# Soft-MoE kernel on one core: stage-2 chunks set between linear steps, dispatch spectra turned on chip

## The chip, the core and the metric

One core of a Trainium2 chip runs the whole program. The metric is device time in microseconds (us), from launch to end; the profile adds one execution taken apart by engine. TensorE does matmuls, VectorE (DVE) and ScalarE (ACT) read its results out of PSUM, GpSimd (POOL) works on SBUF alone, SyncE (SP) issues most DMAs. Each engine works through its own list in order and waits on semaphores for the others.

## What is computed

The reference, cut:

```python
X = np.fft.rfft(x, axis=1)                     # x: (8, 3072, 256)
Yr = Xr @ w_r - Xi @ w_i + b_r                 # complex linear step
Yi = Xr @ w_i + Xi @ w_r + b_i
Yr, Yi = soft_threshold(Yr, 0.01), soft_threshold(Yi, 0.01)
y = np.fft.irfft(Yr + 1j * Yi)                 # (8, 3072, 256) -> 24576 rows
logits = y @ phi                               # 32 slots
d = softmax over rows;  slot_input = d.T @ y   # 8 experts, 4 slots each
slot_out = relu(slot_input @ w1[e]) @ w2[e]
c = softmax over slots; z = c @ slot_out
h = z @ w_in;  out = (h * tanh(softplus(h))) @ w_out
```

## The kernel before

The spectral part takes about the first third, the feed-forward part (the lines behind 820) the rest. Only the spectral part is touched. It goes through eight batches (b = 0 to 7), each in four steps, k = 4b to 4b + 3; a step holds eight residues q of the transform. In outline, for a batch:

- Stage 1 (line 186): six groups of matmuls; ScalarE copies them to `a`, and SP stores them to DRAM, `sdr` (line 216). SP loads `bt` from there, one load a step (line 221, `load_b`, two buffers).
- Stage 2 (line 224): for step k, six chunks (two halves h of the channels, residues in groups of 3, 3 and 2). A chunk's matmuls go to a PSUM bank; ScalarE copies it, rounded, to `xh` (line 240) and VectorE writes what is left over to `xl` (line 241). Both hold two buffers. In a batch's first step, two bins that are real are copied in SBUF as well, on VectorE, once for `xh` and once for `xl` (line 244).
- Linear (line 247): six linear steps for step k, two output halves times three products m. Each is six matmuls, three that read half 0 of `xh` and `xl` and three that read half 1. For m = 0 ScalarE copies the result; for m = 1 and 2 VectorE adds (line 277), ScalarE makes two passes (lines 283, 284) and GpSimd subtracts (line 285) into `yt`. The tile `cl` has one buffer, so ScalarE's first pass waits for GpSimd's subtraction of the linear step before.
- Then `project` (line 290, the logits' spectrum), `inv1` (line 301) and `ytrans` (line 313, y turned by TensorE).
- Once a batch: the inverse transform of the logits (`sturn`, `inv2`), both softmaxes (`smax1` to `smax3`, `csoft1`, `cexp`, `csoft2`), and the forward transform of the dispatch weights: `fwd1` (line 425), `d_load` (line 442), `fwd2` (line 472), `dturn` (line 482), and `slots` (line 487), which sums y with them.

For batches 0 to 6, `fwd1` copies its two results on ScalarE, and SP writes them to DRAM (`ddr`, line 440); `d_load` is one DMA that reads them back with the residues turned onto another axis, in runs of 128 bytes (line 445). Batch 7 has another path: VectorE transposes PSUM in blocks of 32 x 32 into `dm` (line 433), TensorE turns that (line 453), and ScalarE and VectorE copy one half each (lines 458, 456).

The order of the work is written out by hand: every piece has a position (`at`, line 75), the pieces are sorted by it, and each engine's list follows that order. Step k's linear steps stand at k, k + 1/6, ..., k + 5/6; stage 2 of step k stands at k - 1.1, its six chunks 0.0002 apart, so all before linear step (k - 1, 0) and one step ahead of their use; `load_b` at k - 1.91; stage 1's groups in batch 1 at 4.05 - 3.9 + 0.195 (2i + 1), the last at 2.295. `fwd1` stands at 4b + 5.84, `d_load` at 4b + 6.05, `fwd2` at 4b + 6.46 to 6.76. The numbers are in `PA` (line 798) and, for the last batch, `TAIL` (line 801). All PSUM tiles of this part share eight banks, handed round in the order of the program.

Of the kernel before, what the change touches and what calls it, by code (L numbers as in the profile page):

```python
# [8 lines left out]
F32 = mybir.dt.float32  # L9
# [3 lines left out]
AF = mybir.ActivationFunctionType  # L13
# [6 lines left out]
N1, N2 = 128, 24  # L20
R1, R2 = 64, 48
NP = 32
NC = 384
NS = 32
# [44 lines left out]
def body(ctx, tc, x, w_r, w_i, b_r, b_i, phi, w1, w2, w_in, w_out, cbig, ct, out, dbg=None, stop=False):  # L69
    nc = tc.nc  # L70
    NB = x.shape[0]
# [3 lines left out]
    def at(pos, fn, *a):  # L75
        items.append((round(pos, 4), len(items), fn, a))

    dram = ctx.enter_context(tc.tile_pool(name="dram", bufs=1, space=DRAM))
# [3 lines left out]
    f1, f1t, ident, sel = cb[:, 0:128], cb[:, 128:256], cb[:, 256:384], cb[:, 384:416]  # L82
# [7 lines left out]
    def lpool(name, bufs=1, **k):  # L90
        return left.enter_context(tc.tile_pool(name=name, bufs=bufs, **k))
# [3 lines left out]

    const, yp, cp, sm = lpool("const"), lpool("yp", PA["y"]), lpool("cp"), lpool("sm", 2)
    bp = ctx_r.enter_context(tc.tile_pool(name="bp", bufs=2, side="right"))
# [6 lines left out]
    def psum(shape, name):  # L104
        return psp.tile(shape, F32, tag="p", name=name)
# [17 lines left out]
    cs_t = {}  # L123

    x_t, b_t, xh_t, xl_t, yt_t, y_t, pt_t, k1_t = {}, {}, {}, {}, {}, {}, {}, {}
    sdr, spt, ddr, ch, a_t = {}, {}, {}, {}, {}
    XC = 512
    na = N2 * D // XC

# [94 lines left out]
    def stage2(k, h, p0):  # L224
        b, g = divmod(k, 4)
        n = min(3, 8 - p0)
        if h == 0 and p0 == 0:
            xh_t[k] = bp.tile([128, 2, 3 * NC + 48], F32R, tag="xh", name="xh")
            xl_t[k] = bp.tile([128, 2, 3 * NC + 48], F32R, tag="xl", name="xl")
        full = psum([128, 3, 3, 48], "s2")  # L230
        ps = full[:, 0:n]
        for i in range(n):
            nc.tensor.matmul(ps[:, i], lhsT=b_t[k][:, p0 + i, h * 128:(h + 1) * 128], rhs=t_m[:, 8 * g + p0 + i, :],  # L233
                             start=True, stop=True)

        def part(t):
            return t[:, h, 144 * p0:144 * (p0 + n)].rearrange("p (q r f) -> p q r f", r=3, f=48)

        xh = part(xh_t[k])
        nc.scalar.activation(out=xh, in_=ps, func=AF.Copy)  # L240
        nc.vector.tensor_sub(part(xl_t[k]), ps, xh.bitcast(F32))  # L241
        if g == 0 and p0 == 0:
            for t in (xh_t[k], xl_t[k]):
                nc.vector.tensor_copy(t[:, h, 3 * NC:3 * NC + 48].rearrange("p (a r) -> p a r", r=2),
                                      t[:, h, 95:144:48][:, None, :].to_broadcast([128, 24, 2]).bitcast(F32))

    def linear(k, eh, m):
        if eh == 0 and m == 0:
# [176 lines left out]
    def fwd1(b):  # L425
        d = ch[b, 1]
        last = b == NB - 1
        dm = cp.tile([128, 32, N2] if last else [128, N2, NS], F32, tag="st" if last else "chl", bufs=1 if last else 2, name="dm")
        for i in range(2):
            ps = psum([128, 12, NS], "dps")  # L430
            nc.tensor.matmul(ps, lhsT=f1, rhs=d[:, 12 * i:12 * i + 12], start=True, stop=True)
            if last:
                nc.vector.transpose(out=dm.rearrange("p q n -> p n q")[:, 12 * i:12 * i + 12], in_=ps)
            else:
                nc.scalar.activation(out=dm[:, 12 * i:12 * i + 12], in_=ps, func=AF.Copy)
        if last:
            ch[b, 0] = dm
            return
        ddr[b] = dram.tile([NP, 96, NS], F32, tag="ddr", bufs=2, name="ddr")
        nc.sync.dma_start(out=ddr[b].rearrange("q (r n) s -> (q r) n s", r=4), in_=dm)  # L440

    def d_load(b):
        if b < NB - 1:
            dd = cp.tile([96, NP, NS], F32, tag="dd", name="dd")
            nc.sync.dma_start(out=dd, in_=ddr[b].rearrange("q p s -> p q s"))
            ch[b, 0] = [dd[:, q] for q in range(NP)]
            return
        src = ch[b, 0].rearrange("p (c r) n -> p c (r n)", r=4)
        ch[b, 0] = [None] * NP
        for a in range(2):  # L450
            ps = psum([96, 4, 128], "td")
            for c in range(4):
                nc.tensor.transpose(ps[:, c], src[:, 4 * a + c], ident)
            dd = yp.tile([96, 4, 128], F32, tag="y", name="dd")
            if a:
                nc.vector.tensor_copy(dd, ps)
            else:
                nc.scalar.activation(out=dd, in_=ps, func=AF.Copy)
            for c in range(4):
                for g in range(4):  # L460
                    ch[b, 0][8 * g + 4 * a + c] = dd[:, c, 32 * g:32 * g + 32]
# [102 lines left out]
    def s1pos(b, j):  # L564
        if b < 2:
            return -5 + 0.05 * j if b == 0 else 0.15 + 0.195 * j
        if b == 2:
            return 2.5 + 0.305 * j
        return 4 * b + PA["s1"] + PA["s1d"] * j

# [10 lines left out]
    for k in range(NK):  # L581
        at(-4 + 0.01 * k if k < 2 else 2.45 if k == 4 else k + PA["lb"], load_b, k)
        for i, (h, p0) in enumerate((h, p0) for h in range(2) for p0 in (0, 3, 6)):
            at(k + PA["s2"] + PA["s2d"] * i, stage2, k, h, p0)
        for i in range(6):
            at(k + i / 6, linear, k, i // 3, i % 3)
        at(k + PA["pj"], project, k)
        at(k + PA["pj"] + 0.3, inv1, k)
        for c in range(3):
            at(k + PA["yt"] + PA["ytd"] * c if k < NK - 4 else NK + TAIL["yt"][k - NK][c], ytrans, k, c)  # L590
    def pos(n, b):
        t = TAIL.get((n, b - NB))
        return 4 * b + 4 + PA[n] if t is None else NK + t

    for b in range(NB):
        f2 = pos("f2", b)
        for n, f in (("tu", sturn), ("i2", inv2), ("m1", smax1), ("m2", smax2), ("m3", smax3), ("f1", fwd1), ("c1", csoft1),
                     ("ce", cexp), ("ds", dsum), ("dl", d_load), ("c2", csoft2)):
            at(pos(n, b), f, b)
        for g in range(4):  # L600
            at(f2 + 0.1 * g if b < NB - 1 else NK + TAIL["f2"][g], fwd2, b, g)
            at(f2 + 0.1 * g + 0.15 if b < NB - 1 else NK + TAIL["dt"][g], dturn, b, g)
        if b < NB - 2:
            at(pos("sl", b), slots, b)
        else:
            for g in range(4):
                at(NK + TAIL["sl"][b - NB][g], slots, b, (g,))
        for g in range(2):
            at(pos("cx", b) + PA["cxd"] * g, ctrans, b, g)
# [23 lines left out]
    with tc.manual_schedule():  # L633
# [11 lines left out]
        ps = psum([128, 2, NS], "sip")  # L645
# [149 lines left out]
                nc.vector.tensor_copy(sot[:, h, 16 * g:16 * g + 16].rearrange("p (j i) -> p j i", i=SPE), src)  # L795


PA = dict(y=20, s1=-5.89, s1d=0.3402, lb=-1.91, s2=-1.1, s2d=0.0002, pj=1.18, yt=2.24, ytd=0.0002, tu=0.482, i2=1.17, m1=1.17, m2=1.34, m3=1.51, f1=1.84, c1=1.58, ce=1.58, ds=2.47, dl=2.05, c2=2.57, f2=2.46, sl=3.2, rc=0.3, cx=3.24, cxd=0.0002, x0=-0.79, x1=0.05, ytl=1.05, x2=1.3, x3=2.7)


TAIL = {
# [172 lines left out]
```

## Time and profile before

| what | us |
|---|---|
| median of 3 runs | 1934.07 (1930.87 to 1936.53) |
| the profiled execution | 1935.8 |
| its span, first to last instruction | 1934.0 |
| busy in the span: TensorE | 1875.3 (97%) |
| VectorE | 1163.1 (60%) |
| ScalarE | 860.5 (44%) |
| GpSimd | 195.3 (10%) |

Busy times are sums over the whole span; a stage's own limit has to be read from that stage. A TensorE that is busy need not run at its peak, and its granted clock has two levels, 1.2 and 2.4 GHz, shown as 0.50 and 1.00. In a row, "x32" counts instructions, a pair in square brackets is the engine's idle time in front of the row and what ended it, and an fp32 matmul shows as two instructions.

### The profile page before, as it was taken

What the parts mean: (1) busy time and instruction counts of PE and PEld (TensorE: products, weight loads), DVE (VectorE), ACT (ScalarE), POOL (GpSimd) and SP (SyncE); (2) the same over time, 40 slices, a digit from 0 to 9 for tenths busy, and PEclk for the clock granted to TensorE, in tenths of its full rate; (3) what the DMA queues carried; (4) which work ended last, traced back from release to release, by engine and by line L of the source; (5) the groups of instructions that cost most, each with busy time, mean ns of one, the idle gap of its engine ahead of it and who ended that gap; (6) DMA issues with size and microseconds to landing.
All of it is one profiled execution on the core that took longest, in us unless ns stands there. A gap on an engine that the chain in (4) does not pass through costs nothing.

```text
span 1934.0 us, 29831 instructions
## 1 busy us (share of the span) xinstructions
PE 1875.3 (97%) x12106; PEld 1569.4 (81%) x12106; DVE 1163.1 (60%) x1810; ACT 860.5 (44%) x1380; POOL 195.3 (10%) x247
## 2 busy tenths in 40 slices
PE   6899999998998899999999999999999999999999
PEld 4687787777887488888888888888888888888887
DVE  3355655655566476666666666666666666666665
ACT  2666666665754243333333333333333333333332
POOL 0333333332332000000000000000000000000000
PEclk9999999999999999999999999999999999999999
DMA  9867777775663920020020020002002001000000
GB/s 246 235 150 173 168 184 177 170 185 132 161 167 107 343 74 22 23 55 22 12 55 23 23 55 23 23 12 55 22 23 55 22 19 48 22 23 22 23 22 23
DMA packets 96905, 164.28 MB, mean 85 GB/s; under 512 B 28784, under 2 KB 58096, under 8 KB 94848
## 3 DMA queue, kind: packets, MB, share of 16 engines
q1 hardware_dynamic: 93808, 155.13, 29.2%
q0 software_dynamic: 1792, 4.76, 0.8%
q10 hardware_dynamic: 1168, 2.49, 0.5%
q8 instruction: 95, 1.56, 0.3%
q14 instruction: 42, 0.34, 0.1%
HBM read 98.78 MB, written 63.57 MB: 84 GB/s over the span
## 4 chain that ended last, share of the span: by engine, by line
PE 88%; DMA 4%; DVE 3%; ACT 2%; issue 2%; POOL 1%; SPq 0%; POOLq 0%; ACTq 0%; DVEq 0%
PE o L910 56%; PE h L868 9%; PE l L265 8%; PE s L233 6%; PE tr L318 2%; PE s L201 2%; DMA dd<-ddr 2%; DMA bt<-sdr 1%; PE pp L296 1%; DMA xc<-in_x_dram 1%; PE sps L496 1%; POOL yt L285 1%; PE dt L478 1%; ACT cl L283 1%; PE iu L307 1%
## 5 line engine op out<-in xcount | busy, mean ns | idle before, releaser
L910 PE MATMUL o<-whl,gh 128*128 128x512 f32 x3072 | 1082.9, 395 | 0.0
L910 PE MATMUL o<-whl,gl 128*128 128x256 f32 x3072 | 827.9, 280 | 0.0
L881 ACT ACTIVATE g<-h 128x1024 f32<-128x1024 f32 (+1 forms) x385 | 394.2, 1025 | 747.8 <-PE h L868 738.0
L910 PEld LDWEIGHTS o<-whl,gh 128*128 128x128 f32 x3072 | 566.5, 188 | 121.5
L910 PEld LDWEIGHTS o<-whl,gl 128*128 128x128 f32 x3072 | 578.5, 188 | 31.5
L894 DVE TENSOR_TENSOR gl<-g,gh 128x1024 fp32r<-128x1024 f32 x383 | 468.9, 1224 | 29.2 <-DVE gh L887 1.4
L887 DVE CAST gh<-g 128x1024 fp32r<-128x1024 f32 (+1 forms) x385 | 265.8, 690 | 352.6 <-ACT g L881 352.6
L868 PE MATMUL h<-ctt,mst 128*128 128x512 f32 x768 | 240.7, 394 | 1.5 <-ACT g L881 1.0
L233 PE MATMUL s<-tall,bt 96*128 96x144 f32 x1024 | 143.0, 301 | 23.0 <-DMA bt<-sdr 12.1
L233 PEld LDWEIGHTS s<-tall,bt 96*128 96x128 f32 x1024 | 138.6, 202 | 31.0 <-issue 26.4
L241 DVE TENSOR_TENSOR xl<-s,xh 128x432 fp32r<-128x432 f32 (+1 forms) x192 | 94.6, 550 | 113.6 <-ACT xh L240 113.3
L285 POOL TENSOR_TENSOR yt<-cl,p 128x384 f32<-128x384 f32 x124 | 125.2, 1010 | 352.6 <-ACT p L284 220.2
L868 PEld LDWEIGHTS h<-ctt,mst 128*128 128x128 f32 x768 | 121.0, 188 | 19.7 <-ACT g L881 1.8
L283 ACT ACTIVATE cl<-p,tup 128x384 f32<-128x384 f32 x124 | 76.3, 615 | 134.0 <-DVE p L277 98.1
L918 DVE TENSOR_TENSOR os<-o,os 128x256 f32<-128x256 f32 x192 | 76.5, 419 | 77.2 <-ACT os L917 77.2
L277 DVE TENSOR_TENSOR p<-l,k 128x384 f32<-128x384 f32 x128 | 70.6, 553 | 85.2 <-PE l L265 61.9
L240 ACT ACTIVATE xh<-s 128x432 fp32r<-128x432 f32 (+1 forms) x192 | 79.0, 503 | 36.7 <-PE s L233 36.3
L917 ACT ACTIVATE os<-o 128x256 f32<-128x256 f32 x192 | 73.4, 383 | 41.5 <-PE o L910 37.7
L284 ACT ACTIVATE p<-p,tlo 128x384 f32<-128x384 f32 x124 | 76.3, 615 | 4.0
L201 PE MATMUL s<-xc,f 64*64 64x512 f32 x384 | 56.6, 650 | 9.6 <-DMA xc<-in_x_dram 9.5
L318 PEld LDWEIGHTS tr<-cb,yt 128*128 128x128 f32 x384 | 55.4, 235 | 12.0 <-issue 4.5
L318 PE MATMUL tr<-cb,yt 128*128 128x128 f32 x384 | 62.2, 306 | 0.0
(187 smaller groups left out, 1392.1 us busy)
## 6 DMA issues: line engine op xcount, KB each, us to landing
sdr<-a SPq DMA_DIRECT2D x96, 256.0 KB, 3.8
bt<-sdr SPq DMA_DIRECT2D x32, 768.0 KB, 8.5
out_dram<-os SPq DMA_DIRECT2D x47, 512.0 KB, 2.6
xc<-in_x_dram SPq DMA_DIRECT2D x90, 256.0 KB, 5.4
ctt<-c_d SPq DMA_DIRECT2D x28, 384.0 KB, 7.0
w1t<-in_moe_w_dram SPq DMA_DIRECT2D x6, 1024.0 KB, 7.4
c_d<-chl SPq DMA_DIRECT2D x14, 384.0 KB, 2.8
w2t<-in_moe_w_dram SPq DMA_DIRECT2D x5, 1024.0 KB, 12.2
```

Source lines behind the costliest of these rows:

```text
L201: nc.tensor.matmul(ps[h][64 * c:64 * c + 64], lhsT=f64[hs], rhs=t[hs, XC * c:XC * c + XC], start=True, stop=True, tile_position=(64 * h, 6 ...
L233: nc.tensor.matmul(ps[:, i], lhsT=b_t[k][:, p0 + i, h * 128:(h + 1) * 128], rhs=t_m[:, 8 * g + p0 + i, :], start=True, stop=True)
L241: nc.vector.tensor_sub(part(xl_t[k]), ps, xh.bitcast(F32))
L265: nc.tensor.matmul(full[:, 0:48 * nq].rearrange("p (q f) -> p q f", f=48), lhsT=ww[:, h, es], rhs=spec(xx, h), start=n == 0, stop=n == 5)
L283: nc.scalar.activation(out=cl, in_=p, func=AF.Relu, bias=tup[:, ri, eh:eh + 1])
L285: nc.gpsimd.tensor_sub(yt[:, eh, :, ri, :], cl, p)
L318: nc.tensor.transpose(ps[:, i, eh], yt[:, eh].rearrange("p q r f -> p (q r f)")[:, 2 * c + i::6], ident)
L868: nc.tensor.matmul(ps[:, i], lhsT=mst[:, f * 128:f * 128 + 128], rhs=ct_t[b][:, 4 * m:4 * m + 4].rearrange("p n t -> p (n t)"), start=True ...
L881: nc.scalar.activation(out=v(g), in_=v(h), func=AF.Mish)
L887: nc.vector.tensor_copy(v(gh), v(g))
L894: nc.vector.tensor_sub(gl, g, gh.bitcast(F32))
L910: nc.tensor.matmul(o, lhsT=a[:, i, ts], rhs=w, start=f == 0 and n == 0, stop=f == 15 and n == 1)
```

## The change

Three edits. Stage 2's chunks are spread: the first stands at k - 1.03 and each next one 1/6 later, so one stands in front of each of the linear steps of step k - 1. Batches 0 to 6 take the path that batch 7 had (transposes by VectorE and TensorE, `d_load` at 4b + 6.20 instead of 6.05), and the DRAM tensor and its two DMAs a batch are gone. The real bins are read from PSUM: ScalarE writes `xh`'s, VectorE subtracts for `xl`'s.

```diff
@@ stage2 @@
         if g == 0 and p0 == 0:
-            for t in (xh_t[k], xl_t[k]):
-                nc.vector.tensor_copy(t[:, h, 3 * NC:3 * NC + 48].rearrange("p (a r) -> p a r", r=2),
-                                      t[:, h, 95:144:48][:, None, :].to_broadcast([128, 24, 2]).bitcast(F32))
+            bins = full.rearrange("p q r f -> p (q r f)")[:, 95:144:48][:, None, :].to_broadcast([128, 24, 2])
+            xh, xl = (t[:, h, 3 * NC:3 * NC + 48].rearrange("p (a r) -> p a r", r=2) for t in (xh_t[k], xl_t[k]))
+            nc.scalar.activation(out=xh, in_=bins, func=AF.Copy)
+            nc.vector.tensor_sub(xl, bins, xh.bitcast(F32))
@@ fwd1 @@
-        dm = cp.tile([128, 32, N2] if last else [128, N2, NS], F32, tag="st" if last else "chl", bufs=1 if last else 2, name="dm")
+        dm = cp.tile([128, 32, N2], F32, tag="st" if last else "chl", bufs=1 if last else 2, name="dm")
         for i in range(2):
             ps = psum([128, 12, NS], "dps")
             nc.tensor.matmul(ps, lhsT=f1, rhs=d[:, 12 * i:12 * i + 12], start=True, stop=True)
-            if last:
-                nc.vector.transpose(out=dm.rearrange("p q n -> p n q")[:, 12 * i:12 * i + 12], in_=ps)
-            else:
-                nc.scalar.activation(out=dm[:, 12 * i:12 * i + 12], in_=ps, func=AF.Copy)
-        if last:
-            ch[b, 0] = dm
-            return
-        ddr[b] = dram.tile([NP, 96, NS], F32, tag="ddr", bufs=2, name="ddr")
-        nc.sync.dma_start(out=ddr[b].rearrange("q (r n) s -> (q r) n s", r=4), in_=dm)
+            nc.vector.transpose(out=dm.rearrange("p q n -> p n q")[:, 12 * i:12 * i + 12], in_=ps)
+        ch[b, 0] = dm
@@ d_load @@
         if b < NB - 1:
-            dd = cp.tile([96, NP, NS], F32, tag="dd", name="dd")
-            nc.sync.dma_start(out=dd, in_=ddr[b].rearrange("q p s -> p q s"))
-            ch[b, 0] = [dd[:, q] for q in range(NP)]
-            return
+            both = cp.tile([96, 2, 4, 128], F32, tag="dd", name="dd")
         src = ch[b, 0].rearrange("p (c r) n -> p c (r n)", r=4)
         ...
-            dd = yp.tile([96, 4, 128], F32, tag="y", name="dd")
+            dd = both[:, a] if b < NB - 1 else yp.tile([96, 4, 128], F32, tag="y", name="dd")
@@ PA @@
-s2=-1.1, s2d=0.0002, dl=2.05
+s2=-1.03, s2d=1 / 6, dl=2.2
```

## Rows read from the trace of the kernel before

**Rows 1.** Stretches: length, busy time (instructions) of each engine, clock, DMA.
```profile
0.00:640.00 640.00, 592.22 (x4826) 472.29 (x4826) 353.02 (x807) 387.17 (x788) 193.85 (x246) 0.97 0.69 178
640.00:1934.00 1294.00, 1283.10 (x7282) 1097.09 (x7281) 810.11 (x1004) 473.33 (x593) 1.48 (x1) 1.00 0.12 39
244.00:316.50 72.50, 71.09 (x611) 56.88 (x612) 42.44 (x100) 48.99 (x102) 25.29 (x32) 1.00 0.73 180
254.90:257.20 2.30, 2.30 (x21) 2.27 (x19) 1.23 (x3) 1.42 (x4) 0.00 (x0) 1.00 0.00 0
```

**Rows 2.** Waits: who for whom, us in total, times, longest.
```profile
PE s L233 <- DMA bt<-sdr: 12.1, 3, 6.5
...
PE dt L478 <- DMA dd<-ddr: 9.9, 7, 2.5
```

**Rows 3.** Timeline of TensorE: stage 2 behind one of the three late loads.
```profile
390.36 5.83 PE L233 MATMUL s<-tall,bt 96*128 96x144 f32 x32 [2.38 <-DMA bt<-sdr]
```

**Rows 4.** Stretches at the lower clock (columns as in rows 1).
```profile
91.53:101.77 10.24, 6.04 (x25) 6.07 (x26) 1.90 (x5) 1.85 (x4) 1.56 (x2) 0.50 1.08 273
...
467.00:473.80 6.80, 5.44 (x23) 5.47 (x24) 1.90 (x5) 2.34 (x5) 1.88 (x3) 0.50 0.98 215
...
606.95:610.35 3.40, 3.40 (x39) 2.69 (x38) 2.63 (x5) 0.49 (x1) 1.05 (x2) 0.50 0.10 39
```

**Rows 5.** Tiles `dm`, `dd`: instructions, ns min/median/max, first and last start; who waited.
```profile
L453 PE MATMUL td<-cb,dm x8: 272/273/314, 638.1 to 638.9; 128*96 128x128 f32 x8
L433 DVE STREAM_TRANSPOSE dm<-dps x2: 1143/1152/1161, 635.9 to 636.9; 128x384 f32<-128x384 f32 x2
...
  PEld s L233: 3.9, 6
...
L456 DVE COPY dd<-td x1: 686/686/686, 639.2 to 639.2; 96x512 f32<-96x512 f32 x1
```

**Rows 6.** Timeline around the forward transform of one batch (start, us, engine, line).
```profile
295.27 1.49 PE L431 MATMUL dps<-dx,cb 128*128 128x384 f32 x4
...
296.15 0.84 ACT L395 ACTIVATE lg<-lg 128x768 f32<-128x768 f32 x1 [1.00 <-DVE lg L392]
...
296.90 0.60 ACT L283 ACTIVATE cl<-p,tup 128x384 f32<-128x384 f32 x1
...
299.25 0.61 ACT L283 ACTIVATE cl<-p,tup 128x384 f32<-128x384 f32 x1 [1.11 <-POOL yt L285]
...
300.42 0.85 ACT L435 ACTIVATE dm<-dps 128x384 f32<-128x384 f32 x2
...
302.70 2.88 DVE L241 TENSOR_TENSOR xl<-s,xh 128x432 fp32r<-128x432 f32 x6 [5.45 <-ACT xh L240]
```

**Rows 7.** Chain that ended last, 372 to 400 us: start, us, what.
```profile
377.76 1.82 PE tr L318 x12
379.58 1.06 PE l L265 x6
...
381.38 8.85 DMA bt<-sdr
...
397.26 1.02 PE s L201 x8
...
411.75 3.92 PE s L233 x32
```

**Rows 8.** Timeline of SP's queue: start, us to issue, line.
```profile
375.89 0.50 SPq L445 DMA_DIRECT2D dd<-ddr  x1
376.49 4.79 SPq L183 DMA_DIRECT2D xc<-in_x_dram  x2
...
385.19 1.98 SPq L183 DMA_DIRECT2D xc<-in_x_dram  x2
```

**Rows 9.** Chain that ended last, in front of the wait at 88.9 us.
```profile
84.67 3.55 DMA sdr<-a
```

**Rows 10.** The smallest pass on ScalarE in this part (ns min/median/max).
```profile
L273 ACT ACTIVATE cs<-k,half x32: 278/288/298, 47.5 to 574.8; 128x2 f32<-128x2 f32 x32
```

More of the change, by code (lines that the diff above doesn't have):

```diff
@@ L125, in body @@
     x_t, b_t, xh_t, xl_t, yt_t, y_t, pt_t, k1_t = {}, {}, {}, {}, {}, {}, {}, {}
-    sdr, spt, ddr, ch, a_t = {}, {}, {}, {}, {}
+    sdr, spt, ch, a_t = {}, {}, {}, {}
     XC = 512
@@ L795, in run @@
                 nc.vector.tensor_copy(sot[:, h, 16 * g:16 * g + 16].rearrange("p (j i) -> p j i", i=SPE), src)
-PA = dict(y=20, s1=-5.89, s1d=0.3402, lb=-1.91, s2=-1.1, s2d=0.0002, pj=1.18, yt=2.24, ytd=0.0002, tu=0.482, i2=1.17, m1=1.17, m2=1.34, m3=1.51, f1=1.84, c1=1.58, ce=1.58, ds=2.47, dl=2.05, c2=2.57, f2=2.46, sl=3.2, rc=0.3, cx=3.24, cxd=0.0002, x0=-0.79, x1=0.05, ytl=1.05, x2=1.3, x3=2.7)
+PA = dict(y=20, s1=-5.89, s1d=0.3402, lb=-1.91, s2=-1.03, s2d=1 / 6, pj=1.18, yt=2.24, ytd=0.0002, tu=0.482, i2=1.17, m1=1.17, m2=1.34, m3=1.51, f1=1.84, c1=1.58, ce=1.58, ds=2.47, dl=2.2, c2=2.57, f2=2.46, sl=3.2, rc=0.3, cx=3.24, cxd=0.0002, x0=-0.79, x1=0.05, ytl=1.05, x2=1.3, x3=2.7)
 TAIL = {
```

## The prediction

> **What bounds the kernel now.** I began with the stretches and the granted clock [rows 1]. TensorE is busy 592 of the first 640 us and all but 11 of the 1294 us behind them. The change touches only the first part. One batch in its steady state takes 72.50 us, of which TensorE is busy 71.09, at clock 1.00; the mean of the part is 0.97. So the time is that of one engine's list of work, in its order, plus what it waits, and there is to win some 60 us at the very most: 48 us of idle time in the first 640, and half of the slow stretches below. Then I asked who makes TensorE wait. The waits name two DMAs [rows 2]: the dispatch spectrum read back from DRAM, 9.9 us in 7 waits, and the stage-1 result read back, 12.1 us in three waits. The longest, 6.5 us, stands in front of batch 1's first chunk, one of 2.38 us in front of batch 5's [rows 3], which leaves 3.2 us for the third, in front of batch 6's. Last I looked at the clock: five stretches of 27.2 us together stand at 0.50, the 1.2 GHz level: one of 10.24, one of 6.80 and three of 3.40 us, from 391.90, 538.70 and 606.95, of which the last has its row [rows 4]. The first three in time lie around or just behind the three waits for stage 1, the other two just behind a wait for the spectrum. An instruction paced by the clock loses half of such a stretch.
>
> **The spectra on chip.** For batches 0 to 6 (seven times) the write, the read back and both their issues go. With them go the waits of 9.9 us [rows 2] and, of the two stretches of 3.4 us behind them [rows 4], half: 3.4 us. Together 13.3 us gained. What is late next is the turned spectrum itself, so I follow it. The matmuls stay; the two evacuations move from ScalarE (0.85 us the pair) to two VectorE transposes of 1.15 us [rows 5]. VectorE is free there: it sits idle 5.45 us up to 302.70 [rows 6], so 2.3 us fit, and without this cover they would push the subtractions behind them by 2.3 us a batch, 16 us in all. Eight transposes come onto TensorE: the last batch makes the same eight between 638.1 and 638.9 us, so 0.9 us, with a change of tile shape 1.0 us [rows 5]: 7.0 us for seven batches. Nothing of the step is issued on SP or GpSimd any more, so it is moved past none of their work. The transposes stand at 2.2 instead of 2.05, so behind a projection and in front of three turns of y, a linear step and a stage-1 group, 1.82, 1.06 and about 1.0 us [rows 7], which cover the two copies, the longer 0.69 us on VectorE [rows 5]. I take no wait there; the upper end is today's 13.3 us, all back.
>
> For the clock I charge these transposes nothing: a stretch of 2.30 us in which 18 of 21 instructions are such turns (12 of y, six of the combine weights) stands at clock 1.00, in a batch that does too [rows 1]. One rule of the Trainium skill (TensorE: Matmul & The Clock Gate, Part 4: PE-mode transpose) speaks against it: transposes do not count as a busy TensorE for the clock. By that rule the sum below would be about -6.5 us, by the row -18.3 us.
>
> **SP's queue.** The read back stands right in front of loads of x and of the next batch-but-one's first stage-1 chunk. Behind it two loads of x take 4.79 us to issue, a later such pair 1.98 [rows 8]. The stage-1 load so goes out at 381.38 and takes 8.85 us to land, TensorE begins at 390.36 after 2.38 us of waiting [rows 3, 7]. With the read back gone, SP is free about 0.5 + 2.8 = 3.3 us sooner; the load must also wait until the store issued just ahead of the read back at 375.89 has landed (3.55 us in another such place [rows 9], so 379.4), which leaves 2.0 us, and ScalarE, rid of 0.85 us, is ready for that store sooner. That is the whole wait of batch 5 and most of batch 6's. I take both (2.4 + 3.2 us) and half of the two slow stretches behind them (3.40 + 6.80 us, so 5.1): 5.6 + 5.1, 10.7 us gained. Lower end 0. SP's load for step k also waits until the last chunk of step k-2 has used its buffer, which now stands at k-2.2 instead of k-3.1; the load stands at k-1.91, still behind it, so I add nothing. If SP ran ahead and did wait there, stores and loads of x would queue behind it.
>
> **Chunks between linear steps.** The count of instructions on TensorE stays: 32 for a step, 3.92 us [rows 7]. In the steady state no wait is there to be saved, except that the chunks wait for the banks of the spectrum's evacuation, 3.9 us in six waits [rows 5]: banks are handed round in order, and six chunks in a row come round to them; with linear steps between they come later. I take 3.9 us. In batch 1 the last stage-1 group (position 2.295) now runs ahead of four chunks, 20 of 32 instructions, 2.4 us; behind it hang its copy, the store (3.55 us [rows 9]) and the load that ends the wait of 6.5 us [rows 2]. So this wait begins with the same work done and ends 2.4 us sooner; with 1 us for the slow stretch around it 3.4 us gained (ends 0 and 6.5 + 5.1).
>
> What it costs: today all halves of a step are ready one step before they are used. Afterwards between the last chunk and the linear step that needs it stand only one linear step (1.06 us) and one chunk (0.7 us), 1.8 us; the three products of the first half need none of it, 0.5 us more. The last chunk's own pair of copies is about 0.5 us each (VectorE takes 2.88 us for six; a ScalarE pass over more columns takes 0.60 [rows 6]), 1.1 us with the larger of them. ScalarE however works in order, and in front of this copy stand two passes of the linear step before (1.2 us), whose first can wait for GpSimd (1.11 us) [rows 6]. In the worst step of four (exponentials of both softmaxes) the ScalarE passes of the fifth and last linear steps lie between 296.90 and 300.42, those steps' matmuls end at 295.2. Put into that place: the second exponential ends at 297.0, or 297.6 behind one more subtraction; then come the copy of the chunk before (0.5), two passes (1.25) and the last chunk's copy (0.5), so 299.85, and its subtraction ends near 300.4. TensorE, at 295.2 plus two chunks (1.2), the spectrum (1.4), a stage-1 group (1.0), a chunk (0.7) and three products and one more (0.7), wants it near 300.2: a wait of about 0.2 us. I take 0.2 us for 31 steps, 6 us lost. Ends: 0, and the whole pair bare, 1.1 us a step, 34 us.
>
> **Real bins from PSUM.** Per batch four small VectorE copies turn into two small subtractions and two ScalarE passes come; the nearest small pass is 0.29 us [rows 10]. Neither engine is over 68% busy in the batch [rows 1]; price 0, ends 16 x 0.29 = 4.6 us lost (in front of a waiting TensorE each time) and as much gained (the copies that go taken at the same price).
>
> **Sum.** -13.3 -10.7 -3.9 -3.4 +7.0 +6.0 = -18.3 us on the profiled execution of 1935.8: 1917.5. That execution lies 1.7 us over the median of 1934.07, so I forecast 1916 us. A measurement of this kernel can tell about 0.3% (5.8 us) from no change.
>
> **Rivals.**
> 1. Slower: the last chunk. If ScalarE reaches it only when TensorE is already there, in every step, the pair stands bare: 31 x 1.1 = 34 us in place of 6, so 28 more, 1944 us. It decides from (18.3 + 6 + 5.8) / 31 = 1.0 us a step; at 0.8 the gain is gone. For it: ScalarE lagged by 5 us in rows 6. Against: there the exponentials make the lag, and 1.8 us of matmuls and more work cover it. Chance 0.09.
> 2. The stage-1 loads of batches 5 and 6 stay late, because the store's landing and not the queue holds them: 10.7 us back, 1927 us. For it: 8.85 us of flight leaves nothing to spare even in steady batches. Against: 4.79 beside 1.98 us. Chance 0.13.
> 3. The wait for the read back comes again as one for VectorE's transposes or the copies: 13.3 us back, 1929 us. Against: the idle 5.45 us. Chance 0.08.
> 4. The clock: each batch's eight transposes, with the twelve of y behind them, bring one more stretch of 3.4 us at the lower level, so 1.7 us in seven batches, 12 us: 1928 us. Against: the stretch of 2.30 us at 1.00. Chance 0.04. This is the Trainium skill's rule from above (same page and section), as a mechanism of this kernel.
> 5. More: no wait at the last chunk and batch 1's wait nearly gone, 6 + 4 us more: 1906 us. Chance 0.08.
>
> **How the numbers follow.** The forecast has 0.58. Faster by over 0.3% means under 1928.3: the forecast, rival 5, most of rival 2 and half of rival 4, 0.77. Within 0.3%: rival 3 and the rest of 2 and 4, 0.14. Slower: 0.09. The range 1905 to 1930 holds rivals 2 to 5 and most of the forecast's own spread (costs between 0 and 0.5 us a step).
>
> **What would show it.** Right: no DMA of the spectrum, no TensorE wait in front of its last products, the waits for stage 1 at batches 5 and 6 under 1 us, batch 1's near 4 us, two or three slow stretches fewer, 1294 us behind 640 unchanged. Wrong: linear steps that wait for the subtraction of the last chunk by over 0.8 us a step, or waits for the turned spectrum.

## The result and the profile after

The changed kernel takes 1953.73 us (median of four runs, 1952.21 to 1956.79) against 1933.05 us for the kernel before (four runs as well): ratio 1.0107, 95% interval [1.0087, 1.0128]. Slower by 20 us where 18 us less were forecast. The profiled execution took 1953.12 us, its span is 1951.3.

The stretches of the changed kernel, columns as in [rows 1]; the third is one batch, to be read beside the 72.50 us of before:

```profile
0.00:657.30 657.30, 611.47 (x4882) 476.37 (x4882) 367.27 (x812) 385.34 (x797) 194.30 (x246) 0.98 0.63 165
657.30:1951.30 1294.00, 1282.93 (x7282) 1097.95 (x7281) 810.05 (x1004) 473.35 (x593) 1.48 (x1) 1.00 0.12 39
251.66:327.31 75.65, 73.91 (x618) 57.82 (x617) 44.50 (x101) 48.80 (x102) 25.55 (x32) 1.00 0.62 156
```

From the experts' first matmul to the end it takes 1282.6 us before and 1282.7 us after (span less the first line of the table below), so all of the loss lies ahead of it. In one batch TensorE is busy 73.91 us instead of 71.09 and the batch takes 3 us more, at full clock; a wait inside a group of matmuls shows partly as busy time.

The waits of the changed kernel (us in total, times, longest):

```profile
DVE xl L241 <- ACT xh L240: 223.8, 152, 11.9
ACT cl L284 <- DVE p L278: 167.8, 117, 4.2
PEld l L266 <- ACT xh L240: 22.3, 23, 2.2
PE l L266 <- ACT xh L240: 15.1, 18, 1.9
PE s L233 <- DMA bt<-sdr: 4.2, 1, 4.2
```

Both DMA waits of [rows 2] are gone or small: none for the spectrum, one of 4.2 us for stage 1 (batch 1) where there were three. In their place TensorE's linear steps wait for ScalarE's copy to `xh`. And the chain that ended last now leaves TensorE more often; its shares of the whole span, before and after:

```profile
PE 88%; DMA 4%; DVE 3%; ACT 2%; issue 2%; POOL 1%; SPq 0%; POOLq 0%; ACTq 0%; DVEq 0%
PE 79%; ACT 8%; DVE 8%; issue 3%; DMA 2%; SPq 0%; POOL 0%; POOLq 0%; ACTq 0%; DVEq 0%
```

The clock, to be read beside [rows 4]: between 60 and 650 us three slow stretches of 17 us together instead of five of 27 us.

```profile
72.80:79.60 6.80, 6.37 (x20) 4.11 (x21) 1.30 (x4) 2.95 (x5) 1.56 (x2) 0.50 1.00 286
96.70:103.50 6.80, 5.12 (x19) 5.15 (x20) 2.22 (x4) 1.23 (x3) 1.56 (x2) 0.50 1.02 292
212.75:216.10 3.35, 3.35 (x14) 3.35 (x13) 1.22 (x2) 2.34 (x5) 1.88 (x3) 0.50 0.97 212
```

To see where TensorE's time went I added up, in each trace, the time from a matmul's start to the next one's start, by the tile that the first one writes, up to the experts' first matmul. A wait so counts to the work in front of it or inside it. "First linear" is the time from the first to the last of the six matmuls of each step's first linear step, 32 of them. All in us:

| | before | after | e1 | e2 | e3 | e4 | e8 | e9 | e10 |
|---|---|---|---|---|---|---|---|---|---|
| up to the experts | 651.4 | 668.6 | 698.9 | 633.7 | 657.7 | 656.5 | 655.1 | 660.3 | 661.0 |
| linear | 250.5 | 272.9 | 275.8 | 241.6 | 245.5 | 251.4 | 229.9 | 264.1 | 242.8 |
| first linear alone | 32.3 | 62.5 | 52.0 | 32.3 | 34.2 | 41.7 | 32.0 | 54.1 | 34.4 |
| stage 2 | 138.3 | 126.0 | 134.2 | 128.1 | 132.5 | 126.6 | 131.8 | 125.9 | 126.9 |
| stage 1 | 64.1 | 60.6 | 81.7 | 60.8 | 62.5 | 61.6 | 61.5 | 61.6 | 62.6 |
| projection | 30.7 | 33.7 | 32.4 | 31.2 | 40.3 | 40.7 | 60.7 | 33.0 | 51.1 |
| spectrum turned | 0.9 | 7.3 | 0.9 | 7.2 | 7.3 | 7.3 | 7.2 | 7.3 | 7.3 |

The changed kernel gains 12 us at stage 2 and 3.5 us at stage 1, pays 6.4 us for the turned spectra, and loses 30 us in the first linear steps alone: 0.97 us a step over the 31 that have a chunk in front. The other linear steps together take 8 us less, so the whole linear row rises by 22 us.

### The profile page after: what moved, and what is told of

Same layout as the page of the kernel before. It is cut to its first block, busy times and chain, and to the rows that moved or that the text cites. A ratio compares the mean times of both kernels' runs of the same rounds, so it can differ in the third digit from the quotient of the medians.

```text
span 1951.3 us, 29907 instructions
## 1 busy us (share of the span) xinstructions
PE 1894.4 (97%) x12162; PEld 1574.3 (81%) x12162; DVE 1177.3 (60%) x1815; ACT 858.7 (44%) x1389; POOL 195.8 (10%) x247
## 4 chain that ended last, share of the span: by engine, by line
PE 79%; ACT 8%; DVE 8%; issue 3%; DMA 2%; SPq 0%; POOL 0%; POOLq 0%; ACTq 0%; DVEq 0%
PE o L901 55%; PE h L859 9%; PE l L266 4%; PE s L233 3%; ACT cl L284 2%; DVE p L278 2%; ACT xh L240 2%; PE s L201 2%; DVE xl L241 2%; ACT p L285 2%; PE tr L319 1%; DMA bt<-sdr 1%; ACT y L324 1%; PE pp L297 1%; ACT a L207 1%
## 5 line engine op out<-in xcount | busy, mean ns | idle before, releaser
L241 DVE TENSOR_TENSOR xl<-s,xh 128x432 fp32r<-128x432 f32 (+1 forms) x192 | 106.4, 555 | 224.2 <-ACT xh L240 223.8
L233 PE MATMUL s<-tall,bt 96*128 96x144 f32 x1024 | 166.3, 297 | 12.3 <-issue 6.6
L233 PEld LDWEIGHTS s<-tall,bt 96*128 96x128 f32 x1024 | 147.7, 195 | 35.7 <-issue 18.5
L284 ACT ACTIVATE cl<-p,tup 128x384 f32<-128x384 f32 x124 | 76.4, 616 | 172.2 <-DVE p L278 167.8
L240 ACT ACTIVATE xh<-s 128x432 fp32r<-128x432 f32 (+1 forms) x192 | 92.7, 484 | 27.8 <-PE s L233 27.7
L266 PE MATMUL l<-xh,ah 128*128 128x384 f32 (+1 forms) x128 | 53.8, 420 | 15.2 <-ACT xh L240 15.1
```

Source lines behind the costliest of these rows:

```text
L266: nc.tensor.matmul(full[:, 0:48 * nq].rearrange("p (q f) -> p q f", f=48), lhsT=ww[:, h, es], rhs=spec(xx, h), start=n == 0, stop=n == 5)
L284: nc.scalar.activation(out=cl, in_=p, func=AF.Relu, bias=tup[:, ri, eh:eh + 1])
```

## The experiments

**Which edit costs.** e1 and e2 split the change: e1 has only the spread chunks, e2 everything but them. The difference between before and e1, and between the changed kernel and e2, is the same line:

```diff
-s2=-1.1, s2d=0.0002
+s2=-1.03, s2d=1 / 6
```

> The kernel before with one edit: stage 2's chunks spread, one in front of each linear step; spectra through DRAM and real bins as before. Theory A (the last chunk: the first linear step of each step of k waits about 1 us for the split of the chunk in front of it, 30 us in 31 steps): slower than before by 15 to 28 us, 1948 to 1961 us, the first linear steps at 60 us in sum against 32 before. Rival B (the spectra on chip cost the time, by their eight transposes, their VectorE work and ScalarE copies): within 6 us of before, 1927 to 1939 us.

> The changed kernel with the chunks back together (six in a row, a whole step ahead); spectra on chip and real bins from PSUM stay. Theory A: faster than before, by 10 to 17 us, 1916 to 1923 us: the waits for the spectrum's read back and those for stage 1 in batches 5 and 6 stay away, seven times 1 us of transposes is added. Rival B: slower than before, 1940 to 1955 us.

e1: 1984.03 us, 1.0267 [1.0252, 1.0283]. e2: 1919.52 us, 0.9937 [0.9921, 0.9953]. So the spectra on chip with the real bins are a gain of 14 us, and the spread turns it into a loss: 34 us between e2 and the changed kernel, 50 us between before and e1. Rival B has fallen. The first linear steps of e1 are at 52 us, where theory A had 60, yet its time lies above theory A's range, since the two edits hang together. Its waits show one way:

```profile
PE dt L478 <- DMA dd<-ddr: 28.2, 7, 6.3
```

Without six chunks in one piece between the forward transform and its use, the read back through DRAM is waited for 28.2 us instead of 9.9 [rows 2], which the table shows at stage 1, whose group stands in front of that wait. The read back itself is no slower, 6.3 us to landing (median) beside 6.2 us: TensorE comes to it sooner. The path on chip takes this wait away. The clock is the other: each of these seven waits has a slow stretch around or just behind it, as here behind the one that ends at 409.13.

```profile
409.90:420.10 10.20, 10.20 (x84) 7.94 (x86) 5.21 (x13) 1.55 (x3) 0.31 (x1) 0.50 0.76 197
```

Between 60 and 650 us e1's slow stretches come to 65 us, against 27 before. Half of the 38 us more, 19 us, is an estimate of the most that this cost; no run tells it from the waits.

e2 in its trace: one wait for a stage-1 load is left, in batch 1, and the clock is full from 101.7 to 633 us, with all transposes of the spectra in that stretch:

```profile
PE s L233 <- DMA bt<-sdr: 7.3, 1, 7.3
```

```profile
101.70:633.00 531.30, 521.94 (x4516) 419.87 (x4515) 340.78 (x754) 344.74 (x713) 175.25 (x217) 1.00 0.62 166
```

**The real bins alone.** e5 puts the diff's first hunk into the kernel before.

> The kernel before with the real bins read from PSUM, nothing else. Both theories: within 3 us of before (1930 to 1937 us); 16 small ScalarE passes come, 16 small VectorE copies go, none in front of a waiting TensorE.

1934.58 us beside 1934.55, 1.0003 [0.9991, 1.0015]: nothing, as expected. So e2's gain is the spectra's.

**Taking the wait at the last chunk away, in three ways.** e3 sets the chunks closer, so that three linear steps follow the last one:

```diff
-s2=-1.03, s2d=1 / 6
+s2=-1.03, s2d=0.1
```

e4 lets VectorE make the last chunk's copy to `xh`, so that it isn't behind ScalarE's passes:

```diff
+        if h == 1 and p0 == 6:
+            nc.vector.tensor_copy(xh, ps)
+        else:
+            nc.scalar.activation(out=xh, in_=ps, func=AF.Copy)
```

e10 moves the last chunk alone, by one linear step:

```diff
-at(k + PA["s2"] + PA["s2d"] * i, stage2, k, h, p0)
+at(k + PA["s2"] + PA["s2d"] * i if i < 5 else k - 0.35, stage2, k, h, p0)
```

> The changed kernel with the chunks 0.1 of a step apart instead of 1/6: the first still in front of the first linear step, the last in front of the fourth, so three linear steps lie between the last chunk and its use. Theory A: the wait at the first linear step goes, 22 to 30 us less than the changed kernel, 1923 to 1932 us. Rival B: within 6 us of the changed kernel, 1948 to 1960 us. A third view, C (any spreading costs, by the change of matmul kinds on TensorE between chunk and linear step): within 6 us of the changed kernel as well, but with the first linear steps at 32 us.

> The changed kernel with one edit: the last chunk of each step (half 1, two residues) is copied to xh by VectorE instead of ScalarE, so that this copy does not stand behind ScalarE's two passes of the linear step before. Theory A in its narrow form (ScalarE's order makes the wait): 15 to 28 us less than the changed kernel, 1926 to 1939 us. Form A2 (the pair of copies itself is too long, or VectorE is the late one): under 8 us less, 1946 to 1954 us. Rival B: no change.

> The changed kernel with only the last chunk of each step set one linear step earlier (two linear steps between it and its use instead of one). Theory A+: the sum of the first linear steps falls from 62 to 36 to 46 us, a part comes back at the projection (34 to 37 to 41 us), so 8 to 16 us less than the changed kernel, 1938 to 1946 us, and still slower than before. Rival G (the wait is all there is to win back): 26 us or more less, under 1928 us.

e3: 1942.88 us, 1.0052 [1.0035, 1.0068]. e4: 1941.53 us, 1.0049 [1.0032, 1.0065]. e10: 1946.80 us, 1.0076 [1.0051, 1.0102]. In e3 and e10 the first linear steps are nearly as short as before (34.2 and 34.4 us), yet of 28 us only 11 and 7 are won; e4 takes 20.8 us off them and wins 12. So rivals B and G and view C have fallen, but theory A's totals were missed too, in e3 by 11 us and in e4 by 3, where the 12 us lie between its narrow form and A2; in e10 A+ had the kind right and the sizes too small. Not even a small price of changing between kinds of matmuls, a weaker view C, is to be seen in the changed kernel: stage 2 and the linear steps without the first ones come to 336 us there and to 337 us in e2.

The table says where the time went. The projection, 33.7 us in the changed kernel, takes 40.3 us in e3, 40.7 in e4 and 51.1 in e10. Measured against the changed kernel, that is in e4 and e10 most of what came back, 7.0 of 8.7 us and 17.4 of 20.5. In e3 it is 6.6 of 17.4 us; as much came back at stage 2 (6.5), 3.5 at the turns of y, and the forward transform now waits for the exponential:

```profile
PE dps L432 <- ACT dx L385: 8.0, 8, 1.4
```

Here are e10's waits, and its timeline at one projection (start, us, engine, line; in brackets the idle time in front and what ended it):

```profile
PEld pp L297 <- POOL yt L286: 19.5, 17, 2.2
PE pp L297 <- POOL yt L286: 11.3, 12, 1.8
```

```profile
305.85 0.62 ACT L285 ACTIVATE p<-p,tlo 128x384 f32<-128x384 f32 x1
306.56 1.01 POOL L286 TENSOR_TENSOR yt<-cl,p 128x384 f32<-128x384 f32 x1 [5.63 <-ACT p L285]
307.60 0.62 ACT L284 ACTIVATE cl<-p,tup 128x384 f32<-128x384 f32 x1 [1.13 <-DVE dm L433]
308.14 1.05 PE L297 MATMUL pp<-yt,ph 128*32 128x256 f32 x8
308.25 0.61 ACT L285 ACTIVATE p<-p,tlo 128x384 f32<-128x384 f32 x1
308.94 0.99 POOL L286 TENSOR_TENSOR yt<-cl,p 128x384 f32<-128x384 f32 x1 [1.38 <-ACT p L285]
...
309.99 0.63 PE L297 MATMUL pp<-yt,ph 128*32 128x256 f32 x4 [0.79 <-POOL yt L286]
```

The projection needs `yt` of the step's last linear step. Its way there is VectorE's addition, two ScalarE passes and GpSimd's subtraction, one behind the other because `cl` has one buffer. ScalarE's second pair of passes begins at 307.60, when GpSimd's first subtraction has ended (307.57; VectorE's transposes, which the bracket names, end at the same time). GpSimd's second subtraction ends at 309.93 and the projection goes on at 309.99. With the wait at the last chunk taken away, TensorE is ahead of this chain, at 12 projections of 32 in e10, 9 in e4 and 4 in e3.

**What covered the chain before.** If the chunks in one piece, 3.92 us of matmuls in front of the projection's step [rows 7], were what let ScalarE and GpSimd catch up, then moving them whole behind the projection must make it wait, with nothing spread at all. e8 does that to e2:

```diff
-s2=-1.1, s2d=0.0002
+s2=-0.6, s2d=0.0002
```

> The run e2_spectra with the six chunks kept together but moved from the end of a step (-1.1) to behind its third linear step and the projection (-0.6). Theory A+ (the cover): nothing is spread, yet the projection loses its cover: its sum rises from 31 us to 37 to 42 us, the kernel is 6 to 15 us slower than e2_spectra, 1926 to 1935 us; the first linear steps stay at 32 to 34 us. Rival E (the copies of the chunks in between the passes make ScalarE late, not where TensorE's work lies): within 5 us of e2_spectra.

1936.63 us, 1.0012 [0.9999, 1.0024], 17 us above e2 by the medians and a little over the range. The projection takes 60.7 us instead of 31.2, far more than the 37 to 42 expected; the linear steps take 12 us less than in e2 and give part of that back. The first linear steps are at 32.0. Rival E, which had the time within 5 us of e2, has fallen.

```profile
PEld pp L297 <- POOL yt L286: 27.1, 27, 2.2
PE pp L297 <- POOL yt L286: 15.7, 16, 1.8
```

**Moving the one that waits.** e6 is e3 with the projection one linear step later.

```diff
-at(k + PA["pj"], project, k)
+at(k + 1.34, project, k)
```

> The run e3_ahead (changed kernel, chunks 0.1 of a step apart) with the projection moved from 1.18 to 1.34, so behind one more linear step. Theory A+ (with the chunks spread, the ScalarE and GpSimd passes of a step's last linear steps have lost the 3.9 us of stage-2 matmuls that covered them, and the projection, which needs them, waits): the projection falls from 40 us in sum to 30 to 34 us and the kernel is 5 to 10 us faster than e3_ahead, 1933 to 1938 us. Rival D (the lag is spread over everything that ScalarE and VectorE hand to TensorE): the projection falls, but the time is given back at the turns of y or at the banks, within 4 us of e3_ahead, 1939 to 1947 us.

1943.56 us, 1.0047 [1.0031, 1.0062], as e3: A+ missed, and the time lies in rival D's range. The projection falls to 37.4 us only, and what comes behind it, `inv1`, now waits for VectorE's turn of its result:

```profile
PEld iu L308 <- DVE phat L300: 14.7, 13, 2.9
PE iu L308 <- DVE phat L300: 12.9, 14, 2.4
```

This wait is of the edit's own making: `inv1` stayed where it was, so 0.14 of a step is left between the two instead of 0.3, and in e3 TensorE does not wait there. So e6 doesn't tell a lag that lies everywhere (rival D) from one that the move carried to the next hand-over.

**What makes ScalarE late at the last chunk.** e9 takes one thing out of the way in one step of four: the second half of the combine softmax, 2.4 us of VectorE, goes behind the last chunk.

```diff
-c2=2.57
+c2=2.98
```

> The changed kernel with the second half of the combine softmax (csoft2: four VectorE passes, 2.4 us) moved from 2.57 to 2.98, so from in front of the last two chunks to behind them. Theory A (the last chunk's copy stands on ScalarE behind passes that themselves wait for VectorE): the first linear steps behind it (one in four) fall from 2.4 us to 1.4 to 1.8 us, the sum of all first linear steps from 62 to 54 to 58 us, the kernel is 3 to 8 us faster than the changed one, 1946 to 1951 us. Rival F (the pair of copies and its hand-overs alone make the wait): no change in those steps, 1951 to 1957 us.

1946.29 us, 1.0069 [1.0047, 1.0091], 7.4 us less than the changed kernel. The first linear steps behind it fall from 2.43 us to 1.00 us (means of batches 1 to 7), which is no wait at all; the other three stay within 0.2 us of theirs. So theory A holds, more than expected, and rival F falls: the pair of copies itself is short enough when ScalarE is on time. e1 fits this: there TensorE waits for the read back in front of these softmax passes, 2.1 to 6.3 us, and the first linear steps behind them take 1.00 us as well.

**A version that beats both.** e2 is one. e7 sets batch 1's stage-1 groups closer, so that the last one runs ahead of the six chunks of step 3, and batch 1's first stage-1 load earlier (pieces of two lines):

```diff
-return -5 + 0.05 * j if b == 0 else 0.15 + 0.195 * j
+return -5 + 0.05 * j if b == 0 else 0.15 + 0.155 * j
-2.45 if k == 4
+2.1 if k == 4
```

> The run e2_spectra (spectra on chip, real bins, six chunks together) with batch 1's stage-1 groups set closer (0.155 of a step instead of 0.195 apart, so the last stands in front of the six chunks of step 3) and its first stage-1 load at 2.1 instead of 2.45. If the wait of 7.3 us at batch 1 hangs on that last group: 3 to 6 us less than e2_spectra, 1914 to 1917 us. If it hangs on the DMAs' bandwidth: within 2 us of e2_spectra, or slower.

1917.03 us, 0.9903 [0.9886, 0.9920]: the wait of 7.3 us is gone, 2.5 us are won (the intervals of e2 and e7 overlap). The rest came back as a wait of 3.5 us in front of a stage-1 group, from 73.5 us on, with a slow stretch of 10.2 us around its end; e2 has one of 6.8 us in batch 1.

## Why the prediction was wrong

**What held.** The spectra's part: no wait for the read back, transposes at 6.4 us (7.0 forecast), and but one wait for the turned spectrum, 1.1 us for ScalarE's copy in batch 6. SP's queue: at the same place as in [rows 8] the two loads of x now take 1.65 us to issue instead of 4.79, and no load of batches 5 and 6 is waited for:

```profile
389.26 1.20 SPq L216 DMA_DIRECT2D sdr<-a  x2
390.55 1.65 SPq L183 DMA_DIRECT2D xc<-in_x_dram  x2
393.46 0.33 SPq L221 DMA_DIRECT2D bt<-sdr  x1
```

The working had found only 2.0 us for those two waits of 2.4 and 3.2 us, so that both went whole is more than it had shown. The waits at the banks are gone too, in e2, whose chunks stand together, as in e1, whose chunks are spread: either edit takes them. With these 3.9 us and 7.0 us of transposes the terms came to -20.9 us; e2, which has them without the spread, is 14 us faster than before by the medians, and 17 us in the profiled executions (1935.8 and 1918.7), from which the terms were read. In batch 1 the wait fell from 6.5 to 4.2 us, as forecast (2.4 us), but a new wait of 3 us of a stage-1 group at 70 us, with a slow stretch of 6.8 us behind it, took that back. The real bins cost nothing (e5).

**What failed** is the step "a wait of about 0.2 us. I take 0.2 us for 31 steps, 6 us lost". It measures 30 us in the first linear steps, 34 us in all (the changed kernel less e2); some 5 us of the 34 at most are the clock's, an estimate: behind 60 us and ahead of the experts, e2 has 7 us of slow stretches and the changed kernel 17. That comes nearest to rival 1, which had 0.09, and it went past that rival's price too (28 us more than the forecast, 1944 us). The kind was another, though: rival 1 had the last chunk's pair of copies bare in every step, 1.1 us. A batch's first step hardly waits and its last two wait for 1.4 us, so that the mean comes near 1.1 us is luck. Two things were wrong in the step.

First, the working for the place around 300 us lacked a link. I put ScalarE's two passes straight behind its copy of the chunk before. The same place after the change, VectorE, ScalarE and TensorE in order of time:

```profile
305.17 0.84 ACT L396 ACTIVATE lg<-lg 128x768 f32<-128x768 f32 x1 [1.00 <-DVE lg L393]
305.92 0.51 ACT L240 ACTIVATE xh<-s 128x432 fp32r<-128x432 f32 x1
306.46 0.61 DVE L241 TENSOR_TENSOR xl<-s,xh 128x432 fp32r<-128x432 f32 x1 [1.33 <-ACT xh L240]
306.99 0.55 DVE L278 TENSOR_TENSOR p<-l,k 128x384 f32<-128x384 f32 x1
307.90 0.61 ACT L284 ACTIVATE cl<-p,tup 128x384 f32<-128x384 f32 x1 [1.48 <-DVE p L278]
308.20 0.44 PE L266 MATMUL l<-xh,ah 128*128 128x384 f32 x1
308.55 0.62 ACT L285 ACTIVATE p<-p,tlo 128x384 f32<-128x384 f32 x1
309.07 0.39 ACT L240 ACTIVATE xh<-s 128x288 fp32r<-128x288 f32 x1
309.50 0.46 DVE L241 TENSOR_TENSOR xl<-s,xh 128x288 fp32r<-128x288 f32 x1 [1.96 <-ACT xh L240]
309.52 0.45 PE L266 MATMUL l<-xh,ah 128*128 128x384 f32 x1 [0.52 <-ACT xh L240]
```

ScalarE's copy of the fifth chunk ends at 306.43, its first pass begins at 307.90: nearly 1.5 us in which VectorE first subtracts for that very chunk and then adds for the linear step. I had charged nothing for them; with them TensorE sits idle for 0.52 us in front of the first matmul that reads the last chunk's `xh`, its next one waits for `xl`, and the six take 2.1 us instead of about 1 from first to last. A chunk set between two linear steps puts VectorE behind ScalarE, and ScalarE behind VectorE, in turn. With chunks in one piece this happened about once a step. VectorE's waits for ScalarE's copies are now 223.8 us in 152 times and ScalarE's for VectorE's additions 167.8 us in 117; before they were:

```profile
DVE xl L241 <- ACT xh L240: 113.3, 46, 11.8
ACT cl L283 <- DVE p L277: 98.1, 72, 3.5
```

Second, that place was not the only bad one. In batches 1 to 7 the first linear steps take 1.16, 1.94, 2.36 and 2.43 us on the mean for the four steps of a batch, about 1 us where nothing waits; the second exponentials stand in front of the third (the place above), and the fourth, which I had not followed, has the softmax passes on VectorE in front. There:

```profile
326.01 0.96 DVE L406 TENSOR_TENSOR lg<-lg,cs__3412 128x768 f32<-128x768 f32 x1
...
327.18 0.57 DVE L241 TENSOR_TENSOR xl<-s,xh 128x432 fp32r<-128x432 f32 x1
327.68 0.54 DVE L278 TENSOR_TENSOR p<-l,k 128x384 f32<-128x384 f32 x1
...
328.31 0.62 ACT L284 ACTIVATE cl<-p,tup 128x384 f32<-128x384 f32 x1 [4.24 <-DVE p L278]
328.96 0.61 ACT L285 ACTIVATE p<-p,tlo 128x384 f32<-128x384 f32 x1
329.48 0.39 ACT L240 ACTIVATE xh<-s 128x288 fp32r<-128x288 f32 x1
...
329.92 0.44 PE L266 MATMUL l<-xh,ah 128*128 128x384 f32 x1 [1.08 <-ACT xh L240]
```

ScalarE sits idle for 4.24 us, although it is busy for 48.80 us of 75.65: its order, not its load, makes TensorE wait. e9 shows that this one chain is worth 7 us; e4, which takes the last chunk's copy out of ScalarE's list, takes 20.8 of the 30 us off the first linear steps.

Behind this lies a sentence of the first part that was true and misled: that in the steady state no wait is there to be saved. I took the six chunks in one piece as neutral, since TensorE's list keeps its length. They were the cover under which ScalarE and GpSimd brought the last linear steps' `yt` to the projection (e8: 17 us for losing it). I had priced the last chunk's distance from its use, but not what the 3.92 us had hidden where they stood. In the changed kernel the projection takes only 3 us more, as TensorE has already waited in the first linear step. This is also why none of the mended spreads paid: with the wait at the last chunk gone it is next at the projection (e3, e4, e10), and with the projection moved at `inv1` (e6).

What stays open: e2's gain is 7 us short of the sum of its terms by the medians, 4 us in the profiled executions, and no run splits it further. The 5 us that the clock gave back in the changed kernel (an estimate, half of 27 less 17 us of slow stretches) are in the times above and weren't tried by themselves. No run gave `cl` a second buffer or joined two of the mends, so whether some spread could pay is not shown.

## What to carry to other kernels

When work of the bounding engine is moved and its amount stays, ask first what that stretch was hiding: which chain on the other engines ran under it, and who needs that chain's end next. Before setting pieces between one another, write the order of every engine that evacuates them, link by link; two engines that take turns inside each piece add up their hand-overs, and idle shares of a third on each say nothing about it. And try the parts of a change by themselves: here one part was worth 14 us and another lost 34.

## What the runs showed of the hardware

The transposes of the spectra leave the clock alone. In e2 the clock is 1.00 from 101.7 to 633 us with all 56 of the new ones in that stretch, and in the changed kernel none of the three slow stretches lies at one of them by its start (the first of them come at 159 us, the next batch's at 238 us; the stretch at 212.75 follows a first linear step that waited 1.37 us). So rival 4 fell, and the rule of the Trainium skill (TensorE: Matmul & The Clock Gate, Part 4: PE-mode transpose) made no difference here: these are groups of eight between matmuls, and no run has a long stretch of transposes alone.

A DMA of 3072 runs of 128 bytes was dearer at its neighbours than by itself: its own issue took 0.50 us [rows 8], the next two loads' issue 4.79 instead of 1.65 us (3.71 to 5.71 us in the four batches where such a pair follows, 1.65 to 1.79 us at the same places without it), and the packets under 512 bytes were 28784 in the whole execution and are 7056.
